# Natural token order for the attention queries, whole-tile output transfers, and more accumulation banks for layer 2's first products

## The chip, the cores and the metric

The kernel runs on one core of one Trainium2 chip. The metric is the device time of one execution in microseconds (us). Three executions of the kernel before gave 834.37, 836.23 and 836.92 us; the median is 836.23 us.

## The reference, cut to what matters

Nystroem attention over 4 batches, 8 heads, 576 tokens and 64 channels a head is followed by two feed-forward layers over the 2304 tokens (512 channels, 2048 hidden).

```python
q_lm = q.reshape(B, H, 32, S // 32, D).mean(axis=3)     # landmarks: means of 18 tokens each
k_lm = k.reshape(B, H, 32, S // 32, D).mean(axis=3)
A, Bm, C = sm(q, k_lm), sm(q_lm, k_lm), sm(q_lm, k)     # softmaxes of scaled products
Z = ...                                                 # 6 Newton steps towards the inverse of Bm
x = (A @ Z @ C @ v).transpose(0, 2, 1, 3).reshape(2304, 512)
h = x @ moe_w_in;   x = (h * tanh(softplus(h))) @ moe_w_out      # layer 1 (Mish)
h = x @ moe2_w_in;  out = (h * sigmoid(h)) @ moe2_w_out          # layer 2 (SiLU)
```

The result is 2304 rows of 512 numbers, 2 KB a row, in the order (batch, token).

## The kernel before, in words

**Order of the work.** Nothing is scheduled on the chip. While the program is built, a planner (`Line`) keeps an estimated time for each engine, runs generators ("chains") by rank and due time, and so writes each engine's instructions down in one fixed order. Each engine then runs its own list in order and waits on semaphores. The planner counts a transfer as its bytes at a fixed rate plus 2.1 us; what it costs a queue to issue one is not in its estimates. SyncE (SP) issues nearly all transfers, in order; a few at the very end are issued by ScalarE (ACT).

**Attention.** Eight groups (4 batches, 2 halves of the heads) are worked one after another. A group's tokens are loaded with landmark l on the partition: token 18 l + 2 j + e of a head lies at partition l of that head, j from 0 to 8, e from 0 to 1. `transposed` turns them by TensorE (three 128x128 blocks into one PSUM bank) and copies each bank, 384 numbers a partition, to an SBUF tile (`Tk` for keys, `Tq` for queries; in the trace group 1 uses pieces named `wp`). Before the change this tile is laid out by (j, head, l). `scores` reads it as the moving operand, 288 columns for each of 8 matmuls a set: queries as 9 runs of 32 columns, keys with the steps of the pattern that `c_side` asks for, in which neighbouring columns lie 384 numbers (1536 bytes) apart. In groups 2 and 3 (`SUMMED`) the landmarks' sums are made from the same tiles by nine matmuls against `twice`; in the other groups they come from VectorE or GpSimd. The rows of the attention's result, and with them the columns of all later activations, follow the order of the query scores' columns: (batch, e, j, l) before.

**Layer 1** multiplies hidden blocks of 128 with 288 tokens; its output goes to DRAM (`ys`) and comes back for layer 2 by `inputs` in three tiles of 768 tokens. `inputs` makes four loads a tile, two into `xs` buffers and two into `wst` buffers (the ring that also takes weights); the loads of tile t+1 are issued while tile t is worked. The first VectorE instruction on them is the subtraction of the two loads in `wst`.

**Layer 2** replaces 8 products of blocks by 7 (`PRODUCTS`). A turn is one pair of hidden blocks: 7 products of 6 matmuls with 384 columns each (`first_products`, names `h<-...` in the trace), and for the pair of the turn before 12 units of 3 matmuls with 512 columns (`second_products`, names `y<-...`). There are 8 turns in each of 3 tiles. In the first turn of all there is no pair before, so the 7 products stand alone. Each takes a PSUM bank from the ring `h_r`, which has two banks; `combined` adds the banks up on VectorE (`z<-h,z`) and only then gives the bank back. The ring `y_r` has four banks from layer 1 and two more in layer 2; one tile's six results collect there.

**Results.** When a tile of 768 tokens is done, `result` copies each of its six banks (128 tokens, 512 numbers) to one of four SBUF buffers `ysb`, and `send` writes it to the result as four transfers of 32 tokens, because 32 neighbouring columns are the 32 landmarks of one (e, j), 18 tokens apart. In the last tile VectorE copies the left half and ScalarE the right half of a bank, and the four transfers are issued in turn by SP and ACT.

Of the kernel before, what the change touches and what calls it, by code (L numbers as in the profile page):

```python
# [35 lines left out]
    S=(2, 0.2, 0.05),  # L36
# [308 lines left out]
class Ring:  # L345
# [12 lines left out]
    def any(self):  # L358
        return any(p[1] for p in self.pools)
# [47 lines left out]
def kernel(  # L407
# [512 lines left out]
    def first_products(t, turn, p):  # L920

        for name, n in PRODUCTS:
            await_(lambda: h_r.any() and (t, name) in x_t and (t, p, name) in f_t)
            bank = h_r.take([128, 512], FP32)
            x, w_ = x_t[t, name], f_t.pop((t, p, name))
            for k in range(2):
                for m, (i, j) in enumerate(PASSES):
                    T.matmul(
                        out=bank[0][:, 0:TH],
                        lhsT=w_[0][:, i, k * 128:k * 128 + 128],  # L930
                        rhs=x[:, k, j],
                        start=(k == 0 and m == 0),
                        stop=(k == 1 and m == 2),
                    )
                    if m != 1 and k + m < 3:
                        yield 0, None
            if turn < HF - 1 or t == NB[2] - 1:
                Ring.give(w_)
            else:
                f_t[t + 1, p, name] = w_  # L940
            if turn == HF - 1:
                marks.add(("x", t, name))
            yield n, combined(t, p, name, bank)
# [110 lines left out]
    def result(t, d):  # L1054

        y_ = y_t[2, t][d]
        yield from until(ysb_r.any)
        ysb_ = ysb_r.take([128, DM], FP32)
        if t < NB[2] - 1:
            VA.copy(out=ysb_[0], in_=y_[0])  # L1060
        else:
            for i, e in enumerate((V, A)):
                e.copy(out=ysb_[0][:, 256 * i:256 * i + 256], in_=y_[0][:, 256 * i:256 * i + 256])
        Ring.give(y_)
        yield "W"
        send(t * 2 * TH // 128 + d, ysb_[0])
        Ring.give(ysb_)

    def send(r, ysb):

        for i in range(128 // LM):
            b, n = divmod(r * (128 // LM) + i, J)
            e, j = divmod(n, J2)
            rows = out[b * S:(b + 1) * S, :].rearrange("(l j e) d -> e j l d", e=2, j=J2)[e, j]
            late = r * 128 >= NT - 2 * TH and i % 2
            line.transfer(nc.scalar if late else nc.sync, out=rows, in_=ysb[i * LM:(i + 1) * LM, :])


    actx = ctx.enter_context(ExitStack())
    qkv_p = actx.enter_context(tc.tile_pool(name="qkv", bufs=2, side="right"))  # L1080
# [10 lines left out]
    class Group:  # L1091
# [55 lines left out]
        def transposed(self, nm, src):  # L1147
            g = self.g
            if g == 1:
                t = self.borrowed["qk".index(nm) + 1][0][:, 0:J].rearrange("p (j a) (c l) -> p j (a c) l", a=2, l=LM)  # L1150
            else:
                t = t_p.tile([128, J2, HG, LM], FP32, tag="T" + nm, name="T" + nm)
            self.tT[nm] = t
            for j in range(0, J2, 3):
                yield from until(self.banks.open)
                pt = self.banks.take([128, 3, 128], FP32)
                for i in range(3):
                    T.transpose(
                        out=pt[0][:, i, :],
                        in_=src[:, 2 * (j + i):2 * (j + i) + 2, :].rearrange("p a d -> p (a d)"),  # L1160
                        identity=ident,
                    )
                yield "W"
                VA.copy(out=t[:, j:j + 3].rearrange("p j h l -> p j (h l)"), in_=pt[0])
                Ring.give(pt)
                if j + 3 < J2:
                    yield "T+"
            yield "W"
            marks.add((g, "T" + nm))
# [15 lines left out]
        def main(self):  # L1185
            g = self.g
            if g in SUMMED:

                yield from until(marked((g, "Tk"), (g, "Tq")))
                yield from until(self.banks.open)  # L1190
                pl = self.banks.take([128, 2, 128], FP32)
                for i, nm in enumerate("kq"):
                    yield from until(marked((g, "T" + nm)))
                    for j in range(J2):
                        T.matmul(
                            out=pl[0][:, i, :],
                            lhsT=twice,
                            rhs=self.tT[nm][:, j].rearrange("p h l -> p (h l)"),
                            start=(j == 0),
                            stop=(j == J2 - 1),  # L1200
                        )
                    marks.add((g, "lm" + nm))
                    if not i:
                        yield "T"
            else:
                yield from until(marked((g, "lmk"), (g, "lmq")))
                yield from until(self.banks.open)
                pl = self.banks.take([128, 2, 128], FP32)
                for i, nm in enumerate("kq"):
                    lm = self.lm[nm].rearrange("p a d -> p (a d)")  # L1210
                    T.transpose(out=pl[0][:, i, :], in_=lm, identity=ident)
# [143 lines left out]
        def c_side(self):  # L1355
            g = self.g
            yield from until(marked((g, "lmT"), (g, "Tk")))
            yield from until(lambda: self.pairs.open(2))
            kT = self.tT["k"]
            s_, s_c = self.scores(  # L1360
                1, lambda e, h: kT[64 * e:64 * e + 64, :, h, :].rearrange("p (c w) l -> p w l c", c=VC)
            )
            marks.add((g, "sc"))
            yield "V+"
            nm2 = s_p.tile([128, 2], FP32, tag="nm2", name="nm2")
            for e in range(2):
                V.tensor_reduce(out=nm2[:, e:e + 1], in_=s_c[e], axis=AX.X, op=ALU.max)
            yield "V"
            nmc = s_p.tile([128, 1], FP32, tag="nmc", name="nmc")
            V.tensor_reduce(out=nmc, in_=nm2, axis=AX.X, op=ALU.max, negate=True)  # L1370
            yield "A+"
            e_c = a_p.tile([128, 2, SH], FP32, tag="ec", name="ec", bufs=2)
            scr = s_p.tile([128, 1], FP32, tag="scr", name="scr")
            scm = s_p.tile([128, 1], FP32, tag="scm", name="scm")
            sc2 = s_p.tile([128, 2], FP32, tag="sc2", name="sc2")
            for e in range(2):
                A.activation(out=e_c[:, e], in_=s_c[e], func=ACTF.Exp, bias=nmc, accum_out=sc2[:, e:e + 1])
                Ring.give(s_[e])
            line.add(self.total(scm, sc2, scr), self.kind("N"), "V", line.end + 0.17)
            yield "T+"  # L1380
            yield from until(lambda: g == 0 or (g - 1, "cv") in marks)
            ect = a_p.tile([96, VI, 128], FP32, tag="ect", name="ect")
            for i0 in (0, 3):
                yield from until(self.banks.open)
                pe = self.banks.take([96, 3, 128], FP32)
                for i in range(i0, i0 + 3):
                    T.transpose(
                        out=pe[0][:, i - i0, :], in_=e_c[:, i % 2, 96 * (i // 2):96 * (i // 2) + 96], identity=ident
                    )
                yield "W"  # L1390
                VA.copy(out=ect[:, i0:i0 + 3, :], in_=pe[0])
                Ring.give(pe)
                yield "T+"
            yield from until(self.banks.open)
            pu_ = self.banks.take([128, D], FP32)
            pu = pu_[0]
            for i in range(VI):
                for h in range(HG):
                    T.matmul(
                        out=pu[32 * h:32 * h + 32],  # L1400
                        lhsT=ect[:, i, 32 * h:32 * h + 32],
                        rhs=self.vn[:, h, i, :],
                        start=(i == 0),
                        stop=(i == VI - 1),
                    )
            marks.add((g, "cv"))
            yield "V"
            yield from until(lambda: (g, "y") in marks and ("w", scr.name) in line.seen)
            VAs.scaled(out=self.yu[:, LM:], in_=pu, scalar1=scr)
            Ring.give(pu_)  # L1410
            yield "W"
            marks.add((g, "u"))
# [9 lines left out]
        def a_side(self):  # L1422
# [1 line left out]
            yield from until(marked((g, "lmT"), (g, "Tq"), (g, "sc")))  # L1424
            yield from until(lambda: self.pairs.open(2))
            qT = self.tT["q"]
            s_, s_a = self.scores(0, lambda e, h: qT[64 * e:64 * e + 64, :, h, :])
            marks.add((g, "scores"))
            if g == 1:
                for t_ in self.borrowed:  # L1430
# [211 lines left out]
```

## Time and profile before

| what | value |
|---|---|
| median of three executions | 836.23 us (834.37 to 836.92) |
| the profiled execution | 835.47 us |
| its span, first to last instruction | 833.3 us |
| TensorE busy | 814.3 us |
| VectorE, ScalarE, GpSimd busy | 560.2, 441.8, 119.5 us |
| mean granted TensorE clock | 0.996 of full speed |

Times in the trace count from the span's start. Attention runs until about 205 us, with layer 1's first work between; layer 1 runs until about 444 us; layer 2 from there. All engines' instructions carry line 262 (the helper that issues them) and all transfers line 274, so they are told apart by the names of their tiles.

### The profile page before, as it was taken

Reading aid. Unit: us, or ns where it says so; the run is one execution under the profiler, and the core shown is the slowest. Engines: PE = TensorE matmul, PEld = TensorE weight load, DVE = VectorE, ACT = ScalarE, POOL = GpSimd, SP = SyncE. Lnnn points to the kernel's source line nnn. Section 1 sums busy time; section 2 is a strip of 40 time slices with the busy share of each in tenths; the row PEclk is TensorE's granted clock in tenths of the full one; section 3 lists DMA queues with packets and bytes.
Section 4 is the critical chain, followed back from the end, with each engine's and each line's share of the span. In section 5 each row is a group of like instructions: output and inputs, shape, how many; then the busy total and the mean of one; then the engine's idle time right before and its main releaser. Section 6 shows DMA issues by size and latency. Waiting matters only on the chain.

```text
span 833.3 us, 15450 instructions
## 1 busy us (share of the span) xinstructions
PE 814.3 (98%) x5920; PEld 729.4 (88%) x5920; DVE 560.2 (67%) x1281; ACT 441.8 (53%) x979; POOL 119.5 (14%) x163
## 2 busy tenths in 40 slices
PE   9999999999999999999998999999999999999997
PEld 7787879878899899999997889888788988988985
DVE  7978875775676879653549998576555567555542
ACT  6466657867566554543436665446445436544422
POOL 2011221030000001000001212211232211232210
PEclk9999999999999999999999999999999999999999
DMA  8784124200175556421143342003100000200002
GB/s 280 234 212 159 58 66 135 87 3 29 32 227 162 183 190 210 145 61 58 57 133 130 103 139 64 0 1 105 48 1 0 1 1 24 53 0 1 1 1 76
DMA packets 41610, 72.30 MB, mean 87 GB/s; under 512 B 4417, under 2 KB 31041, under 8 KB 41537
## 3 DMA queue, kind: packets, MB, share of 16 engines
q1 hardware_dynamic: 40960, 70.53, 27.0%
q8 instruction: 46, 0.75, 0.4%
q10 hardware_dynamic: 576, 0.79, 0.3%
q14 instruction: 28, 0.22, 0.1%
HBM read 57.15 MB, written 14.16 MB: 86 GB/s over the span
## 4 chain that ended last, share of the span: by engine, by line
PE 89%; DVE 5%; DMA 2%; ACT 2%; issue 1%; SPq 0%; ACTq 0%; DVEq 0%
PE y L262 48%; PE h L262 32%; PE t L262 9%; DMA out_dram<-ysb 1%; DMA aw<-in_moe_w_in_dram 1%; DVE m L262 1%; ACT wp L262 1%; DVE z L262 1%; SPq L274 0%; DVE wa L262 0%; DMA kn<-in_k_dram 0%; ACT z L262 0%; ACT ysb L262 0%; ACT L262 0%; DVE xg L262 0%
## 5 line engine op out<-in xcount | busy, mean ns | idle before, releaser
L262 PE MATMUL y<-g,wo 128*128 128x288 f32 x1536 | 227.4, 300 | 1.2 <-DVE g L262 1.1
L262 PEld LDWEIGHTS y<-g,wo 128*128 128x128 f32 x1536 | 208.4, 188 | 13.8 <-issue 11.2
L262 PE MATMUL y<-wo,xg 128*128 128x512 f32 x693 | 180.4, 395 | 0.0
L262 PEld LDWEIGHTS y<-wo,xg 128*128 128x128 f32 x693 | 128.8, 188 | 21.1
L262 DVE TENSOR_TENSOR z<-h,z 128x384 f32<-128x384 f32 x162 | 88.4, 555 | 72.5 <-PE h L262 68.9
L262 PE MATMUL h<-at,wp 128*128 128x288 f32 x768 | 120.0, 301 | 2.7 <-ACT z L262 2.4
L262 PEld LDWEIGHTS h<-at,wp 128*128 128x128 f32 x768 | 105.5, 188 | 12.0 <-issue 7.1
L262 ACT ACTIVATE z<-h 128x288 f32<-128x288 f32 x128 | 51.4, 413 | 65.9 <-PE h L262 64.8
L262 DVE TENSOR_TENSOR g<-z,g 128x288 fp32r<-128x288 f32 x119 | 52.9, 459 | 35.1 <-ACT g L262 31.4
L262 ACT ACTIVATE z<-z 128x384 f32<-128x384 f32 x94 | 49.4, 525 | 32.4 <-DVE z L262 31.9
L262 PE MATMUL h<-xg,wp 128*128 128x384 f32 x288 | 58.1, 336 | 2.3 <-DVE z L262 2.3
L262 PE MATMUL h<-xg,wf 128*128 128x384 f32 x288 | 57.8, 336 | 0.0
L262 PEld LDWEIGHTS h<-xg,wp 128*128 128x128 f32 x288 | 51.2, 188 | 6.2 <-DVE z L262 3.1
L262 DVE TENSOR_TENSOR xg<-z,xg 128x384 fp32r<-128x384 f32 x75 | 42.1, 561 | 20.4 <-ACT xg L262 20.3
L262 ACT CAST g<-z 128x288 fp32r<-128x288 f32 x122 | 50.4, 435 | 8.9 <-PE y L262 7.6
L262 PEld LDWEIGHTS h<-xg,wf 128*128 128x128 f32 x288 | 51.2, 188 | 3.4 <-DVE z L262 0.3
L262 DVE SCALAR_TENSOR_TENSOR m<-wst,m 128x512 int32<-128x512 int32 x64 | 45.3, 708 | 0.7
L262 PE MATMUL y<-wo,wp 128*128 128x512 f32 x171 | 45.2, 396 | 0.0
L262 ACT ACT_TABLE_LOAD x31 | 39.8, 1283 | 8.7 <-DVE nmc L262 3.6
L262 POOL TENSOR_TENSOR g<-z,g 128x288 fp32r<-128x288 f32 x9 | 7.4, 822 | 223.2 <-PE y L262 127.8
L262 ACT CAST xg<-z 128x384 fp32r<-128x384 f32 x75 | 38.4, 513 | 1.5
L262 POOL TENSOR_TENSOR wf<-m,wf 128x256 fp32r<-128x256 f32 x18 | 13.4, 743 | 171.6 <-ACT wf L262 169.9
(237 smaller groups left out, 1171.9 us busy)
## 6 DMA issues: line engine op xcount, KB each, us to landing
wst<-in_moe_w_out_dram SPq DMA_DIRECT2D x32, 512.0 KB, 6.1
wst<-in_moe_w_in_dram SPq DMA_DIRECT2D x22, 512.0 KB, 5.4
kn<-in_k_dram SPq DMA_DIRECT2D x8, 576.0 KB, 6.8
vn<-in_v_dram SPq DMA_DIRECT2D x8, 576.0 KB, 7.1
yh<-ysb SPq DMA_DIRECT2D x32, 144.0 KB, 1.8
ysb<-yh SPq DMA_DIRECT2D x32, 144.0 KB, 2.6
ys<-ysb SPq DMA_DIRECT2D x32, 144.0 KB, 2.2
qn<-in_q_dram SPq DMA_DIRECT2D x7, 576.0 KB, 4.2
```

Of the source, the lines that this page charges most:

```text
L262: r = getattr(self.nc[e], name)(**kw)
```

## The change

1. `transposed` lays the tiles out otherwise. Keys go to (head, w, l, c), so that the scores read 288 neighbouring numbers; the copies write with a step of 3 numbers (12 bytes). Queries go to (head, l, w, c), natural token order within e; the scores read 288 neighbouring numbers and the copies write with a step of 9 numbers (36 bytes). `main` and the two score calls index the new layout; the sums of groups 2 and 3 then read with steps of 3 and 9 numbers.
2. `send` writes what is one run of neighbouring tokens of one (batch, e) in one transfer, every second row of the result: 128 rows where a tile of 128 lies within 288, else two. In tiles 0 and 1 that is one or two transfers of whole rows after the copy, by SP. In tile 2 each half of the columns has its own transfers (1 KB a row): SP's after VectorE's copy, ACT's after ScalarE's.
3. `first_products` may take banks of `y_r` too, in the first turn of the first tile only.

```diff
     def first_products(t, turn, p):
         for name, n in PRODUCTS:
-            await_(lambda: h_r.any() and (t, name) in x_t and (t, p, name) in f_t)
-            bank = h_r.take([128, 512], FP32)
+            rings = (h_r, y_r) if t == turn == 0 else (h_r,)
+            await_(lambda: any(r.any() for r in rings) and (t, name) in x_t and (t, p, name) in f_t)
+            bank = next((r for r in rings if r.ready()), next(r for r in rings if r.any())).take([128, 512], FP32)
...
         if t < NB[2] - 1:
             VA.copy(out=ysb_[0], in_=y_[0])
+            Ring.give(y_)
+            yield "W"
+            send(nc.sync, t * 2 * TH // 128 + d, ysb_[0], 0, DM)
         else:
-            for i, e in enumerate((V, A)):
+            for i, (e, queue) in enumerate(((V, nc.sync), (A, nc.scalar))):
                 e.copy(out=ysb_[0][:, 256 * i:256 * i + 256], in_=y_[0][:, 256 * i:256 * i + 256])
-        Ring.give(y_)
-        yield "W"
-        send(t * 2 * TH // 128 + d, ysb_[0])
+                if i:
+                    Ring.give(y_)
+                send(queue, t * 2 * TH // 128 + d, ysb_[0], 256 * i, 256)
         Ring.give(ysb_)
 
-    def send(r, ysb):
-        for i in range(128 // LM):
-            b, n = divmod(r * (128 // LM) + i, J)
-            e, j = divmod(n, J2)
-            rows = out[b * S:(b + 1) * S, :].rearrange("(l j e) d -> e j l d", e=2, j=J2)[e, j]
-            late = r * 128 >= NT - 2 * TH and i % 2
-            line.transfer(nc.scalar if late else nc.sync, out=rows, in_=ysb[i * LM:(i + 1) * LM, :])
+    def send(queue, r, ysb, at, n):
+        done = 0
+        while done < 128:
+            be, first = divmod(r * 128 + done, SH)
+            rows = min(128 - done, SH - first)
+            to = out[be // 2 * S:be // 2 * S + S, at:at + n].rearrange("(n e) d -> e n d", e=2)[be % 2, first:first + rows]
+            line.transfer(queue, out=to, in_=ysb[done:done + rows, at:at + n])
+            done += rows
...
         def transposed(self, nm, src):
-                t = self.borrowed["qk".index(nm) + 1][0][:, 0:J].rearrange("p (j a) (c l) -> p j (a c) l", a=2, l=LM)
+                t = self.borrowed["qk".index(nm) + 1][0][:, 0:J].rearrange("p j d -> p (j d)")
-                t = t_p.tile([128, J2, HG, LM], FP32, tag="T" + nm, name="T" + nm)
+                t = t_p.tile([128, J * D], FP32, tag="T" + nm, name="T" + nm)
+            if nm == "k":
+                t = t.rearrange("p (h w l c) -> p c w h l", h=HG, w=J2 // VC, c=VC)
+            else:
+                t = t.rearrange("p (h l w c) -> p w c h l", h=HG, w=VC, l=LM)
...
-                VA.copy(out=t[:, j:j + 3].rearrange("p j h l -> p j (h l)"), in_=pt[0])
+                VA.copy(out=t[:, j // 3], in_=pt[0].rearrange("p w (h l) -> p w h l", h=HG))
...
-                            rhs=self.tT[nm][:, j].rearrange("p h l -> p (h l)"),
+                            rhs=self.tT[nm][:, j // 3, j % 3],
...
-                1, lambda e, h: kT[64 * e:64 * e + 64, :, h, :].rearrange("p (c w) l -> p w l c", c=VC)
+                1, lambda e, h: kT[64 * e:64 * e + 64, :, :, h].rearrange("p c w l -> p w l c")
...
-            s_, s_a = self.scores(0, lambda e, h: qT[64 * e:64 * e + 64, :, h, :])
+            s_, s_a = self.scores(
+                0, lambda e, h: qT[64 * e:64 * e + 64, :, :, h].rearrange("p w c l -> p l w c")
+            )
```

## Rows read from the trace of the kernel before

**Rows 1.** The page, busy time of each engine: us (share), instructions.
```profile
PE 814.3 (98%) x5920; PEld 729.4 (88%) x5920; DVE 560.2 (67%) x1281; ACT 441.8 (53%) x979; POOL 119.5 (14%) x163
```

**Rows 2.** Timeline where layer 2 begins: start, us, engine, out<-in, count, [idle before <-releaser].
```profile
444.02 1.22 PE L262 MATMUL h<-x,wf 128*128 128x384 f32 x6
...
448.99 1.31 PE L262 MATMUL h<-xg,wp 128*128 128x384 f32 x6 [0.40 <-DVE z L262]
...
452.44 1.32 PE L262 MATMUL h<-wp 128*128 128x384 f32 x6 [1.09 <-DVE z L262]
...
453.91 1.32 PE L262 MATMUL h<-x,wp 128*128 128x384 f32 x6
```

**Rows 3.** Windows at layer 2's start: span, busy PE, PEld, DVE, ACT, POOL, PEclk.
```profile
450.00:452.00 2.00, 1.35 (x8) 1.03 (x6) 2.00 (x6) 1.20 (x3) 0.03 (x1) 1.00 0.90 327
```

**Rows 4.** Timeline of SP's queue where tile 0's results leave.
```profile
576.89 0.38 SPq L274 DMA_DIRECT2D wst<-ys  x1
577.37 5.60 SPq L274 DMA_DIRECT2D out_dram<-ysb  x12
583.07 0.38 SPq L274 DMA_DIRECT2D wst<-ys  x1
```

**Rows 5.** Timeline of the compute engines there.
```profile
579.57 0.57 ACT L262 COPY ysb<-y 128x512 f32<-128x512 f32 x1
...
585.83 1.56 PE L262 MATMUL y<-wo,wp 128*128 128x512 f32 x6
586.95 0.56 DVE L262 TENSOR_TENSOR wst<-wst 128x384 f32<-128x384 f32 x1 [3.50 <-DMA out_dram<-ysb]
...
588.69 0.55 DVE L262 TENSOR_TENSOR z<-h,z 128x384 f32<-128x384 f32 x1
...
589.30 1.31 PE L262 MATMUL h<-xg,wp 128*128 128x384 f32 x6 [1.91 <-DVE z L262]
```

**Rows 6.** Windows just after it, columns as in rows 3.
```profile
591.00:592.00 1.00, 1.00 (x4) 0.80 (x3) 1.00 (x3) 0.54 (x2) 0.74 (x1) 0.50 0.00 0
```

**Rows 7.** Chain of waits, 570 to 597 us: start, us, what.
```profile
571.67 1.04 PE h L262 x6
572.71 1.41 PE y L262 x6
...
590.61 2.29 PE y L262 x6
592.90 1.72 PE h L262 x6
```

**Rows 8.** Timeline of the last results.
```profile
824.20 0.37 ACT L262 COPY ysb<-y 128x256 f32<-128x256 f32 x1 [5.79 <-DVE ysb L262]
...
824.60 5.67 SPq L274 DMA_DIRECT2D out_dram<-ysb  x12
...
824.96 0.89 ACTq L274 DMA_DIRECT2D out_dram<-ysb  x2
...
829.16 1.75 ACTq L274 DMA_DIRECT2D out_dram<-ysb  x4
```

**Rows 9.** Timeline of group 4's attention, 100 to 120 us.
```profile
105.77 0.47 ACT L262 COPY Tq<-t 128x384 f32<-128x384 f32 x1
...
107.20 0.88 PE L262 MATMUL t<-Tk,lmT 64*32 64x288 f32 x16
...
114.15 0.71 PE L262 MATMUL t<-Tq,lmT 64*32 64x288 f32 x16
```

**Rows 10.** Timeline of group 3's landmark sums of queries.
```profile
69.66 2.17 PE L262 MATMUL t<-Tq,twice 128*128 128x128 f32 x18
```

**Rows 11.** Groups by line and form: count | busy us, mean ns | idle before.
```profile
L262 DVE TENSOR_REDUCE lmk<-kn 128x64 f32<-128x1152 f32 x5 | 11.0, 2193 | 2.9 <-DMA kn<-in_k_dram 2.9
...
L262 DVE TENSOR_REDUCE asm<-at 128x18 f32<-128x576 f32 x8 | 6.0, 748 | 0.8 <-ACT at L262 0.7
```

**Rows 12.** Transfers: out<-in, queue, count, KB each, median us to landing.
```profile
yh<-ysb SPq DMA_DIRECT2D x32, 144.0 KB, 1.8
```

## The prediction

> **What bounds the kernel now.** The page's busy times come first: TensorE is busy 98% of the span, 814.3 of 833.3 us [rows 1]. So nothing on another engine counts unless TensorE waits for it, and all that can be won is in three places: some 19 us in which TensorE is idle, stretches in which its clock is low, and the time after its last product. I then read the chain of waits and the timeline at the places where TensorE stands still, and find three that the change touches.
>
> The first is layer 2's first turn. Seven products of six matmuls run from 444.02 to 453.91 us, where the next turn's first begins [rows 2]: 9.89 us. In steady state six such matmuls take 1.04 us [rows 7], so seven need 7.28. Lost: 2.6 us, of which 0.40 and 1.09 are waits that the timeline names, for `z<-h,z` on VectorE, the instruction that frees a bank of `h_r` [rows 2]. The reader is also to see that VectorE has no gap there: 2.00 us busy of 2.00 between 450 and 452 [rows 3].
>
> The second is at 587 to 594 us. VectorE stands 3.50 us before it subtracts `wst<-wst` at 586.95; its next instructions include the `z<-h,z` of 588.69, and TensorE waits 1.91 us for that, until 589.30 [rows 5]. The row blames a result transfer. But the subtraction needs two loads, and the second sits on SP's queue behind twelve result transfers that take 5.60 us to issue; it goes out at 583.07, right behind them [rows 4]. It lands when the subtraction starts, 3.88 us after its issue began. The data are tile 2's and not urgent, but the instruction is in VectorE's fixed order, and all that TensorE needs next is queued behind it. After the idle time the granted clock is 0.50, the 1.2 GHz level, where it was 1.00 (2.4 GHz) [rows 6], and the chain of waits shows the price: six matmuls of 512 columns take 2.29 us instead of 1.41, six of 384 columns 1.72 instead of 1.04 [rows 7].
>
> The third is the tail. The last results are copied from 824 us on; SP needs 5.67 us to issue twelve transfers, and ACT issues its last four from 829.16 for 1.75 us, to 830.91 [rows 8], while the span ends at 833.3. Two on ACT take 0.89, so 0.44 each.
>
> **The first turn's banks.** The edit adds no instruction; it takes the bank out of the condition. The gain is at most 2.6 us. It is at least 0: VectorE is full [rows 3], and the second turn's products still go to `h_r` alone, so the wait may only move from the third product to the eighth. I take 1.5, the two named waits, because the seven products need no more from VectorE to be issued, and each sum then finds its product ready; what is late next is the next turn's first product, behind VectorE's sums, by the remaining 1.1.
>
> **Tile 0's results.** 24 transfers become 8 (tiles of 128 tokens that cross a multiple of 288 need two; among the first six these are the third and the fifth). SP's queue is otherwise in the same order. Between the two loads it now holds 1 + 2 + 1 transfers instead of 12. The fourth bank's copy starts at 579.57 and takes 0.57 [rows 5], so its transfer goes at about 580.2 and, at 0.47 an issue (5.60 / 12), the load at about 580.65: 2.4 us earlier. Landing 3.88 later it is there at 584.5. VectorE then waits some 1.1 instead of 3.5, and the `z<-h,z` ends at 588.69 + 0.55 - 2.4 = 586.8. TensorE's product before that ends at 585.83 + 1.56 = 587.39 [rows 5], so it finds the sum done. It gains the wait of 1.91, the restart (1.31 - 1.04 = 0.27), and, as the clock has no idle time to fall after, 0.88 + 0.68 = 1.56 of slow matmuls: 3.7 us together. Bounds: 0, if the load stays late, to 3.7. At 2.4 us earlier there are 0.6 us to spare, so I take the whole. Tile 1's results (24 transfers become 8 too) have no such load between them: covered, nothing.
>
> **The tail.** Twelve transfers a queue become eight (two of the last six tiles cross). ACT has six copies of 0.37 and now eight issues of 0.44 instead of twelve: at most 4 x 0.44 = 1.8 us less. But before, an issue ran beside the next tile's copy (the pair at 824.96 sits between copies); now each waits for the copy just ahead of it, some 0.37 that was partly hidden, and with four `ysb` buffers the fifth tile still waits for the first one's transfers. The transfers themselves, 128 KB in pieces of 1 KB, are bounded by a neighbour of 144 KB in rows of 1152 bytes that lands in 1.8 us [rows 12]: no worse than now. Bounds 0 and 1.8, taken 0.9.
>
> **The new layouts.** A key set of scores, 16 records, takes 0.88 us with far-apart columns, a query set with runs of 32 takes 0.71 [rows 9]. Read as one run, keys should cost what queries do: 8 x 0.17 = 1.4 us less. Against it, the landmark sums of groups 2 and 3 now read with steps; a set takes 2.17 us [rows 10]. The step of 1536 bytes cost a factor 0.88 / 0.71 = 1.24, so a stepped set may cost 0.5 more: 1.0 for the two query sets (36 bytes), another 1.0 for the keys (12 bytes), or nothing. I take the queries' 1.0. Net -0.4; bounds -1.4 and +0.6.
>
> The 48 copies write with steps. No row has such a write. The nearest is a stepped read on VectorE: summing 1152 numbers 256 bytes apart takes 2193 ns, while 576 neighbours take 748 [rows 11], so 1152 would take about 1496; 0.6 ns more a number, or 0.23 us for a copy of 384. All 48: 0 to 11 us of mostly ACT time. I take nothing, for two reasons: a store need not be waited for as a read is, and in the groups' middle the delay is covered. Group 4's last query copy ends at 106.2 and TensorE reads it at 114.15 [rows 9], with other work of its own between. Without that cover it would cost up to 0.23 a copy.
>
> The Trainium skill has a rule against this edit: Advanced Engine Details and Errata, section Memory Cachelines, says that SBUF works in lines of 16 bytes, that at least two accesses must fall on a line to hide its latency, and that a pattern with another line each time pays. By that rule the query copies (36 bytes) and their sums pay, and the key scores gain; rows 9 agree with the second half, and no row shows a stepped write. By that rule the sum would lose 24 x 0.23 = 5.6 us wherever the cover fails; as a mechanism it is the slower rival below.
>
> **Sum.** Against the profiled execution's own 835.47 us (span 833.3 and 2.2 around it): -1.5 - 3.7 - 0.9 - 0.4 = -6.5, so 829.0. The median of the runs shown lies 0.76 above that execution; the predicted median is 829.8.
>
> **The rivals.**
> - The stall at 587 stays. For it: the instruction order is written by a planner that knows nothing of issue times, and its estimates shift with the first turn's banks, so the load may come out elsewhere, or another transfer hold it. Against: the planner counts the same bytes for four transfers as for one, so the order should be kept. Then -2.8: 833.4.
> - The first turn gains nothing, since VectorE is the limit there [rows 3] and the wait moves to the eighth product: 831.3.
> - The change does nothing measurable: both stalls stay in another form, and the tail is bound by bytes. Left is 1.3: about 835.
> - Slower: the stepped copies. If both kinds pay the 0.23 and TensorE waits for each, that is 11.0 us over 205 us of attention, and with the second key sums 12: 836.2 - 6.5 + 12 = 841.7. It decides once 6.5 of these 12 us are exposed. For it: the read row. Against: the cover of rows 9, and ACT's spare time (53% busy over the span, rows 1).
>
> **How the numbers follow.** This kernel's measurement can tell about 0.3%, 2.5 us, from no change: the borders are 833.7 and 838.7. Chances: all parts work, with a partial loss here or there, 0.55 (826.8 to 831.5; its best is 836.2 - 2.6 - 3.7 - 1.8 - 1.4); the stall at 587 stays 0.17, about two thirds of it faster; the first turn gains nothing 0.13; nothing measurable 0.08; slower 0.07. Faster 0.55 + 0.11 + 0.13 = 0.79; same 0.06 + 0.08 = 0.14; slower 0.07. The range reaches from the best case to the case with the stall and a little more: 826.5 to 834.
>
> **What would show it.** Right: no named wait between the first seven products, whose span falls from 9.9 to about 8.4 us; the second `wst<-ys` some four issues behind the first; VectorE's wait before `wst<-wst` near 1 us; the clock at 1.00 after it; key and query score sets both near 0.71; ACT's last issue within about 6 us of its first copy. Wrong: `Tq<-t` copies well above 0.47 us with TensorE waits for them before 205 us; a TensorE wait for a `y` bank in the second turn; VectorE still 3 us late at the subtraction; a low clock elsewhere. Most likely to break it is a new order of VectorE's work in layer 2 that puts another early load in its way.

## The result and the profile after

The changed kernel takes 841.79 us (median of six executions, 841.30 to 842.50); the kernel before took 835.42 beside it (six executions, 833.52 to 836.92). The ratio is 1.0078 [1.0063, 1.0092]: slower, where 829.8 was forecast and 834.0 was the upper end. The profiled execution has a span of 839.5 us against 833.3.

Where the time went is read from stages, by the start of the same instruction in both traces:

| stage | before | after | difference |
|---|---|---|---|
| start to the first query scores | 12.36 | 13.37 | +1.01 |
| from there to layer 2's first product | 431.66 | 441.45 | +9.79 |
| layer 2's first turn | 9.89 | 9.32 | -0.57 |
| second turn of tile 1 (the tenth of all) | 19.47 | 15.70 | -3.77 |
| all other turns, 22 of them | 350.37 | 350.37 | 0.0 |
| first copy of the last results to the end | 9.58 | 9.34 | -0.24 |

A turn is timed from the first matmul of its first product to that of the next turn. The stall of [rows 5] lies in the tenth turn, whose first product starts at 579.53 before. The differences add up to 6.22 us, the spans' own. Layer 2 gave 4.6 us; everything lost was lost before it. The first line can't be put down to the change: in six traces with the attention as before (that of before and five of the experiments) it lies between 12.26 and 13.92. The second lies between 431.66 and 432.62 there.

Busy times of the page after, as in [rows 1]:

```profile
PE 819.7 (98%) x5920; PEld 732.7 (87%) x5920; DVE 562.5 (67%) x1280; ACT 451.5 (54%) x977; POOL 122.2 (15%) x166
```

TensorE has the same 5920 instructions and 5.4 us more of busy time; ScalarE has 9.7 us more. So instructions became longer. The groups by form say which (out<-in, count | busy us, mean ns | idle before):

```profile
L262 ACT COPY Tq<-t 128x384 f32<-128x384 f32 x20 | 17.6, 882 | 2.2 <-PE t L262 2.0
...
L262 ACT COPY Tk<-t 128x384 f32<-128x384 f32 x18 | 12.5, 694 | 8.4 <-PE t L262 8.3
...
L262 PE MATMUL t<-Tq,twice 128*128 128x128 f32 x36 | 8.6, 409 | 0.0
...
L262 PE MATMUL t<-Tk,twice 128*128 128x128 f32 x36 | 6.6, 343 | 0.0
```

The same four groups of before had 484, 480, 275 and 275 ns. Now the timeline after: group 2's landmark sums, answering [rows 10], and group 4's scores, answering [rows 9]:

```profile
47.12 3.25 PE L262 MATMUL t<-Tk,twice 128*128 128x128 f32 x18
...
50.47 4.32 PE L262 MATMUL t<-Tq,twice 128*128 128x128 f32 x18
...
116.96 0.72 PE L262 MATMUL t<-Tk,lmT 64*32 64x288 f32 x16
...
123.72 0.71 PE L262 MATMUL t<-Tq,lmT 64*32 64x288 f32 x16
```

A set of sums was 2.17 us; keys now take 3.25, queries 4.32, in each of two groups: 2 x (1.08 + 2.15) = 6.5 us, all of it time in which TensorE itself works. Key scores fell from 0.88 to 0.72, seven sets of them after the first query scores: -1.2. Of the 9.79 us that leaves 9.79 - 6.5 + 1.2 = 4.5 us (4.2 by 432.0, the mean of those six traces) for the copies, which became 24 x 0.40 + 24 x 0.21 = 14.7 us longer in all. How they reach TensorE is in part seen in its waits by releaser, of the first 212 us (us in total, times, longest; those that ScalarE released after the first query scores):

```profile
PE t L262 <- ACT ec L262: 0.5, 2, 0.3
PE t L262 <- ACT ut L262: 0.5, 1, 0.5
...
PE t L262 <- ACT Tq L262: 0.4, 2, 0.2
...
PE h L262 <- ACT yu L262: 0.4, 1, 0.4
...
PE t L262 <- ACT Tk L262: 0.2, 1, 0.2
PE h L262 <- ACT eb L262: 0.2, 1, 0.2
```

Together 2.2 us; before there were two such rows, `yu` 0.3 and `ec` 0.2. Only 0.6 of it names a slower copy: the rest names other results of ScalarE, whose list the copies are part of. But idle time is the small part of the second line. Windows over that stretch, before and after, columns as in [rows 3], then the weight loads' waits for the copies there after; before they were 0.7 for `Tq` and 0.9 for `Tk`:

```profile
12.36:444.02 431.66, 424.07 (x3973) 381.60 (x3958) 302.93 (x779) 246.67 (x560) 32.46 (x36) 1.00 0.39 124
13.37:454.82 441.45, 432.59 (x3973) 387.34 (x3958) 303.48 (x779) 254.63 (x561) 32.43 (x36) 1.00 0.38 121
```
```profile
PEld t L262 <- ACT Tq L262: 2.5, 10, 0.4
...
PEld t L262 <- ACT Tk L262: 1.8, 6, 0.5
```

TensorE's busy time rises by 8.5 us and its idle time by 1.3. Sums and key scores are 5.3 of the 8.5; the other 3.2 lie in matmuls that do the same work as before, so part of the waiting isn't idle time of TensorE and shows in the weight loads ahead of the matmuls. The matmuls of this stretch come in the same order in both traces, so the time from each one's start to the next one's can be compared. Outside the sums and scores these times grew by 4.6 us together: by 2.2 where the next matmul or its weights waited (over 0.15 us) for a copy of `Tq` or `Tk`, by 0.9 where they waited for another result of ScalarE, and the rest is scattered, with no wait of this size.

Layer 2's start in the timeline, answering [rows 2]:

```profile
454.82 1.22 PE L262 MATMUL h<-x,wf 128*128 128x384 f32 x6
...
457.96 1.20 PE L262 MATMUL y<-xg,wf 128*128 128x384 f32 x6
...
464.14 1.33 PE L262 MATMUL h<-x,wp 128*128 128x384 f32 x6 [1.42 <-DVE z L262]
```

The waits of 0.40 and 1.09 are gone, a `y` bank is in use, and one wait of 1.42 has appeared before the eighth product, the first that may not use that ring.

Where tile 0's results leave, SP's queue, answering [rows 4]; VectorE there, answering [rows 5]; and windows, columns as in [rows 3], answering [rows 6]:

```profile
585.40 0.43 SPq L274 DMA_DIRECT2D wst<-ys  x1
586.74 2.80 SPq L274 DMA_DIRECT2D out_dram<-ysb  x4
589.63 0.40 SPq L274 DMA_DIRECT2D wst<-ys  x1
```
```profile
593.90 0.56 DVE L262 TENSOR_TENSOR wst<-wst 128x384 f32<-128x384 f32 x1 [1.21 <-DMA wst<-ys]
```
```profile
590.00:595.00 5.00, 5.00 (x27) 4.60 (x26) 2.75 (x7) 3.21 (x8) 0.73 (x1) 1.00 0.80 241
```

Four issues lie between the two loads instead of twelve; VectorE waits 1.21 instead of 3.50; TensorE has no gap, and its granted clock stays at 1.00.

The last results in the timeline, answering [rows 8]:

```profile
830.66 0.37 ACT L262 COPY ysb<-y 128x256 f32<-128x256 f32 x1 [5.79 <-DVE ysb L262]
...
835.00 1.18 ACTq L274 DMA_DIRECT2D out_dram<-ysb  x2
835.07 0.42 DVE L262 COPY ysb<-y 128x256 f32<-128x256 f32 x1 [1.04 <-ACT ysb L262]
836.23 0.37 ACT L262 COPY ysb<-y 128x256 f32<-128x256 f32 x1 [1.25 <-DVE ysb L262]
836.63 0.34 ACTq L274 DMA_DIRECT2D out_dram<-ysb  x1
```

From the first copy of ScalarE to its last issue's end it is 6.31 us, where it was 6.71. VectorE's last copy now waits 1.04 for ScalarE, and ScalarE's last copy 1.25 for VectorE's.

### The profile page after: what moved, and what is told of

It reads as the page before. It is cut to its first block, busy times and chain, and to the rows that moved or that the text cites. A ratio compares the mean times of both kernels' runs of the same rounds, so it can differ in the third digit from the quotient of the medians.

```text
span 839.5 us, 15401 instructions
## 1 busy us (share of the span) xinstructions
PE 819.7 (98%) x5920; PEld 732.7 (87%) x5920; DVE 562.5 (67%) x1280; ACT 451.5 (54%) x977; POOL 122.2 (15%) x166
## 4 chain that ended last, share of the span: by engine, by line
PE 91%; DVE 4%; ACT 3%; DMA 1%; issue 1%; ACTq 0%; SPq 0%; DVEq 0%
PE y L262 49%; PE h L262 33%; PE t L262 9%; ACT wp L262 1%; DMA kn<-in_k_dram 1%; DVE at L262 1%; DVE m L262 0%; ACT Tq L262 0%; ACT z L262 0%; ACT Tk L262 0%; ACT L262 0%; DVE g L262 0%; DVE st L262 0%; ACTq L274 0%; DVE lmk L262 0%
```

## The experiments

**The theory** after the result (theory S in the expectations): a step between neighbouring numbers costs the engine that makes it, at either end, by how many numbers of a 16-byte piece of SBUF it uses: the sums pay as readers, the copies as writers. **A rival**, called theory C in the expectations: the writes alone pay, and the sums are long only because their copies come late. **Another**: little of it is the layout; what layer 2's edits should have gained went elsewhere.

### Keys as before, queries as before, both

Three kernels from the changed one, each with old storage; the scores keep their column orders, so with old query storage they read numbers 512 bytes apart.

```diff
-                t = t.rearrange("p (h w l c) -> p c w h l", h=HG, w=J2 // VC, c=VC)
+                t = t.rearrange("p (c w h l) -> p c w h l", h=HG, w=J2 // VC, c=VC)
```
```diff
-                t = t.rearrange("p (h l w c) -> p w c h l", h=HG, w=VC, l=LM)
+                t = t.rearrange("p (w c h l) -> p w c h l", h=HG, w=VC, l=LM)
```

> The changed kernel with the keys stored as before (copies write neighbours, scores read 1536 bytes apart); queries as changed. Theory S (every access with a step costs in place: key copies 0.69 instead of 0.48 us, key sums 3.25 instead of 2.17 us a set): the two key sums give back 2.2 us and the key copies about 1.3, the eight key score sets cost 1.3 again: 841.8 - 2.2 = 839.6 us. Theory C (the loss is ScalarE's time for copies; the sums are late only because the copies are): the 24 key copies are a third of the added copy time, so a third of 10.8 us comes back less 1.3: 839.5 us, but with key sums still above 2.17 us a set.

Keys as before (first diff): 839.23 us, 1.0057 [1.0042, 1.0072], about what both theories gave; what tells them apart is the sums. The kernel before had 834.81 beside it in this and the next three runs. The timeline of group 2's sums:

```profile
47.15 2.17 PE L262 MATMUL t<-Tk,twice 128*128 128x128 f32 x18
...
49.42 4.32 PE L262 MATMUL t<-Tq,twice 128*128 128x128 f32 x18
```

The sums of keys are back at 2.17; those of queries stay at 4.32 although nothing of theirs was touched.

> The changed kernel with the queries stored as before and read by the scores in natural order, 512 bytes apart from one column to the next; keys as changed. Theory S: query sums give back 4.3 us, query copies about 3, the eight query score sets cost 0.16 each more, as the keys' did: 841.8 - 7.3 + 1.3 = 835.8 us, query sums at 2.17 us a set and query score sets at 0.88. Theory C: two thirds of 10.8 come back, less 1.3: 835.9 us; what tells them apart is where TensorE falls behind, in the sums or before them.

Queries as before (second diff): 838.52, 1.005 [1.0035, 1.0065], 2.7 us above what was expected. The timeline of group 2:

```profile
46.02 3.24 PE L262 MATMUL t<-Tk,twice 128*128 128x128 f32 x18
...
62.33 1.39 PE L262 MATMUL t<-Tq,lmT 64*32 64x288 f32 x16
```

The sums do as the theory says: keys 3.24, queries back at 2.17. The miss is in the last row: scores that take their columns in turn from nine runs cost 1.39 a set, not the 0.88 of the keys' three runs. Eight sets are 5.4 us where 1.3 were counted; the rest of the kernel gave 1.4 back.

> The changed kernel with both tiles stored as before; only the scores read queries in natural order, 512 bytes apart; output transfers and banks as changed. Theory S and theory C: all 10.8 us come back, the query score sets cost 8 x 0.16: 841.8 - 10.8 + 1.3 = 832.3 us, faster than the kernel before (835.4). A third theory, that the order of the tokens or the output transfers are themselves to blame, expects it to stay slower than before, above 838.

Both as before: 836.38, 1.0023 [1.0013, 1.0033], missed by eight sets at 1.39. From the first query scores to layer 2 it is 437.43 us. That is 4.8 to 5.8 us over the old attention, and the eight query sets, all of them behind that mark, with 0.68 more each are 5.4 of it: between -0.6 and 0.4 is left of the 9.8, which is within the spread, so with the storage goes the loss. Layer 2 stands as in the kernel after (first turn 9.32, tenth 15.70, tail 9.40).

The copies' share follows from the first two in the same way, against the 432.0 us of the old attention. Keys as before: 438.80, less 4.3 for the sums of queries, leaves 2.5 for the copies of queries. Queries as before: 438.97, less 2.15 for the sums of keys and 5.4 for the scores, plus 1.2 for the keys', leaves 0.6 for the copies of keys. Together 3.1, beside the 4.2 to 4.6 above; each of these remainders carries the spread of up to 1.0 us of an unchanged attention.

### Old storage in the two summed groups only

```diff
-                t = t.rearrange("p (h w l c) -> p c w h l", h=HG, w=J2 // VC, c=VC)
+                t = t.rearrange("p (c w h l) -> p c w h l" if g in SUMMED else "p (h w l c) -> p c w h l", h=HG, w=J2 // VC, c=VC)
...
-                t = t.rearrange("p (h l w c) -> p w c h l", h=HG, w=VC, l=LM)
+                t = t.rearrange("p (w c h l) -> p w c h l" if g in SUMMED else "p (h l w c) -> p w c h l", h=HG, w=VC, l=LM)
```

> The changed kernel with both tiles stored as before in groups 2 and 3 alone, where the landmark sums read them; groups 0, 1 and 4 to 7 as changed. Theory S: the four sums give back 6.5 us and the copies of the two groups about 2.1; four score sets cost 0.16 each again: 841.8 - 8.0 = 833.8 us. Theory C: a quarter of the copies, so a quarter of 10.8 us: 839.1 us.

835.43, 1.0006 [0.9997, 1.0016]. Both sums are at 2.17 although the copies of the other six groups are slow as in the kernel after: theory C, with 839.1, falls. The time is 1.6 us above the 833.8 of the first theory; the two groups' query scores, which again come from nine runs, are 1.0 of that (0.68 more a set where 0.16 was counted).

### The step by itself

A small kernel of its own: ScalarE copies 384 and VectorE 192 numbers a partition into a tile with steps of 1 to 16 numbers; TensorE reads 192 columns with the same steps, then 288 columns in turn from 2, 3 and 9 runs that lie 1536 bytes apart. The copies run beside matmuls of the same kernel; only the last groups of matmuls have TensorE to themselves.

> Not the reference's work: copies of a PSUM bank to SBUF with steps of 1, 2, 3, 4, 5, 8, 9 and 16 numbers (384 a partition on ScalarE, 192 on VectorE), matmuls of 192 columns that read SBUF with these steps, and matmuls whose columns go round 2, 3 or 9 runs 1536 bytes apart; nothing else is computed. If a line of 16 bytes costs two accesses' time however little of it is used, the cost of a number follows the lines touched: step 2 free, step 3 at 1.5 times, steps of 4 and more at 2 times and equal; for a matmul 192 columns at those factors. If the cost rises with the step itself, 9 costs more than 4 and 16 more than 9. If only powers of two are bad (banks), 8 and 16 stand out. Runs taken in turn: each column touches another line, so 2 times for all three by the first theory, though the keys' scores before (three runs) took only 1.24 times.

ScalarE's copies with steps 1, 2, 3, 4 and 9 (ns lowest/median/highest of four), then TensorE's groups of 15 matmul records (two records a matmul) with the same steps from the timeline, then those from 2, 3 and 9 runs:

```profile
L44 ACT COPY act<-src x4: 478/478/478, 32.5 to 34.1; 128x384 f32<-128x384 f32 x4
...
L44 ACT COPY act<-src x4: 497/502/512, 34.4 to 36.0; 128x384 f32<-128x384 f32 x4
...
L44 ACT COPY act<-src x4: 666/667/671, 36.4 to 38.5; 128x384 f32<-128x384 f32 x4
...
L44 ACT COPY act<-src x4: 832/835/836, 39.0 to 41.6; 128x384 f32<-128x384 f32 x4
...
L44 ACT COPY act<-src x4: 843/848/899, 49.0 to 51.6; 128x384 f32<-128x384 f32 x4
```
```profile
32.49 2.60 PE L54 MATMUL pe<-big,ident 128*128 128x192 f32 x15
...
35.10 2.71 PE L54 MATMUL pe<-big,ident 128*128 128x192 f32 x15
...
37.89 4.02 PE L54 MATMUL pe<-big,ident 128*128 128x192 f32 x15
...
42.07 5.28 PE L54 MATMUL pe<-big,ident 128*128 128x192 f32 x15
...
58.55 5.35 PE L54 MATMUL pe<-big,ident 128*128 128x192 f32 x15
...
69.24 4.76 PE L61 MATMUL str<-big,ident 128*128 128x288 f32 x15
...
74.17 5.13 PE L61 MATMUL str<-big,ident 128*128 128x288 f32 x15
...
79.61 7.48 PE L61 MATMUL str<-big,ident 128*128 128x288 f32 x15
```

A step of 2 is nearly free (478 and 502 ns; 2.60 and 2.71 us), 3 costs TensorE 1.5 times as much, and 4 and 9 twice; longer ones cost no more (TensorE 5.33 and 5.05 us with 5 and 16, ScalarE 858 and 844 ns with 8 and 16). A copy grows by 0.19 us with step 3 and 0.37 with step 9; in the kernel it was 0.21 and 0.40. VectorE's copies of 192 go the same way: 357, 357, 418, 506 and 506 ns. An access is slow by its own step and not by its neighbour's: VectorE's 357 ns without a step were taken beside matmuls with a step of 8.

The Trainium skill's rule in Advanced Engine Details and Errata, section Memory Cachelines (lines of 16 bytes, two accesses wanted on each), agrees with these rows. The page gives no price; if each line touched is taken to cost the time of two accesses, steps of 1 and 2 put four and two numbers on a line and are free, a step of 3 has 0.75 lines a number and costs 0.75 / 0.5 = 1.5, and a step of 4 or more has one line a number and costs 2.0. TensorE measured 1.04, 1.55, 2.03 and 2.06 for steps of 2, 3, 4 and 9; a whole copy on ScalarE, part of whose time does not grow with the numbers copied (256 take 372 ns, 512 take 586), 1.05, 1.40, 1.75 and 1.77. Several runs in turn are milder than the rule would make them: one run of 288 columns would take an estimated 2.60 x 288 / 192 = 3.9 us, so 2 and 3 runs cost 1.22 and 1.32 times as much, 9 runs 1.92. Without a step all these records take 0.90 ns a column. Layer 2's take 0.45 (1.04 us for 6 of 384), and no run shows what a step does to those.

### The banks alone, and what the stall is worth

The kernel before with the third edit alone:

```diff
-            await_(lambda: h_r.any() and (t, name) in x_t and (t, p, name) in f_t)
-            bank = h_r.take([128, 512], FP32)
+            rings = (h_r, y_r) if t == turn == 0 else (h_r,)
+            await_(lambda: any(r.any() for r in rings) and (t, name) in x_t and (t, p, name) in f_t)
+            bank = next((r for r in rings if r.ready()), next(r for r in rings if r.any())).take([128, 512], FP32)
```

> The kernel before with the first turn's banks alone; layouts, token order and output transfers as before. Theory S (the banks give 0.6 us, the 3.8 us at 587 come from fewer transfers ahead of the second load): 834.8 - 0.6 = 834.2 us, and VectorE's late subtraction and TensorE's wait with it stay. Rival: the banks shift the planner's order so that the load no longer stands behind the results, and the 3.8 us are theirs: 830.4 us.

834.05, 0.9988 [0.9978, 0.9998], the kernel before at 834.84 in this and the next two runs. The first turn takes 9.33 as in the kernel after. VectorE's wait is as it was, and this time the row names the load itself:

```profile
587.12 0.56 DVE L262 TENSOR_TENSOR wst<-wst 128x384 f32<-128x384 f32 x1 [3.48 <-DMA wst<-ys]
```

Its tenth turn is 17.77: in this execution the clock did not fall after the gap, so the stall cost 2.1 us where it cost 3.8 in the profile of before.

### Old token order, whole-tile transfers

To have the fewer transfers without the layouts: old storage and old token order, each transfer's destination written as up to 4 groups of 32 rows (only the lines of the transfers are shown).

```diff
-            to = out[be // 2 * S:be // 2 * S + S, at:at + n].rearrange("(n e) d -> e n d", e=2)[be % 2, first:first + rows]
+            to = out[be // 2 * S:be // 2 * S + S, at:at + n].rearrange("(l j e) d -> e j l d", e=2, j=J2)[
+                be % 2, first // LM:(first + rows) // LM
+            ]
...
```

> The changed kernel with both tiles stored and read as before, so that results come in the old token order; banks as changed; a run of results of one (batch, e) still goes out in one transfer, whose rows in DRAM then follow (j, landmark) in two steps, 2 rows and 36 rows apart... in place of one. Theory S: the 10.8 us of the attention come back whole and the 0.6, 3.8 and 0.3 us of the other parts stay: 834.8 - 4.7 = 830.1 us. Rival: a transfer with four blocks of 32 rows lands later than one with 128 rows in one step, so the tail, or the second load, gives some of it back: 832 to 834.

861.52, 1.0315 [1.0297, 1.0333]: a miss by 31 us, and not in the attention, which is as before (431.74 us). The tenth turn is 26.27, the same turn of tile 2 is 19.73 instead of 15.68, and the tail 24.56. SP's queue in the timeline, then windows in this kernel's tail and in the tail of the kernel after (the last two numbers are the DMA engines' mean busy share and GB/s):

```profile
576.75 5.69 SPq L274 DMA_DIRECT2D out_dram<-ysb  x4
```
```profile
844.00:848.00 4.00, 0.00 (x0) 0.00 (x0) 0.42 (x1) 0.37 (x1) 0.00 (x0) 0.50 0.27 95
```
```profile
833.00:835.00 2.00, 0.67 (x3) 0.19 (x1) 0.42 (x1) 0.98 (x3) 0.00 (x0) 1.00 0.85 290
```

The same bytes move at a third of the rate with a third of the engines' share, so the four buffers come free late and ScalarE, VectorE and TensorE wait behind them. The Trainium skill has this in DMA: Bandwidth & Descriptors, in the section on why a DMA increments its semaphore by 16: a transfer is spread over as many engines, up to 16, as divide the slowest dimension of both sides. With 4 groups outermost that is 4 of 16, and the share of 0.27 agrees. The trace's DMA records speak for it and against slower packets: in both tails most packets have 1024 bytes, and a packet takes 49 ns on average here and 46 in the kernel after, but here mostly four or five are under way at a time, there mostly 13 to 18.

> As e9_old_order, but the second turn of the first tile may take banks of the larger ring too. If VectorE's sums are what the eighth product waits for because VectorE has no time left (busy without a gap there): no change against e9_old_order, within 0.5 us; TensorE's 1.4 us only move on. If it waits for a bank alone: 1.4 us less.

The same kernel with `t == 0 and turn < 2`: 858.51, 1.028 [1.0264, 1.0295]. The first turn falls from 9.33 to 7.74 and the second rises from 15.78 to 16.06: 1.3 us gained, at 1.4 expected if the bank is the limit. (The rest of the 3.0 us lies mainly in the two turns that wait for results, 26.04 and 18.15 instead of 26.27 and 19.73.) VectorE's first four sums start at the same times in both, 2.65, 4.92, 8.73 and 9.3 to 9.5 us after the turn's start; so it is the bank that the eighth product waits for.

### The stall without the layouts

The banks-alone kernel, with the loads' first subtractions placed later in VectorE's order by the planner; the transfers stay 72. Of its diff, the lines that delay the subtraction:

```diff
+            if t:
+                late = line.now + 5.0
+                yield from until(lambda: line.now >= late)
```

> The kernel before with the first turn's banks, and with the planner told to wait 5 us after the loads for tiles 1 and 2 before it places VectorE's first subtraction on them; layouts and the 72 output transfers as before. If the 3.8 us at 587 come from that one instruction standing in VectorE's order before its load has landed: VectorE does not wait, the clock stays, 834.05 - 3.7 = 830.3 us, though SP issues as many transfers as before. If the number of transfers matters in itself (their bytes, their time on SP): 834.

832.61, 0.9969 [0.9958, 0.998]; the kernel before had 834.97 beside it in this and the next three runs. SP's queue and VectorE in the timeline:

```profile
578.48 5.74 SPq L274 DMA_DIRECT2D out_dram<-ysb  x12
584.32 0.39 SPq L274 DMA_DIRECT2D wst<-ys  x1
```
```profile
590.33 0.94 DVE L262 TENSOR_TENSOR wst<-wst 128x384 f32<-128x384 f32 x1
```

The load is as late as ever, behind twelve issues; VectorE no longer waits for it, and the tenth turn falls to 15.93. So the stall was VectorE's fixed order in front of a late load, and it can be taken away at either end. The gain over the banks alone is 1.4 us, not the 3.7 expected; in that kernel's profile the clock did not fall, so only 2.1 us were there to be won.

> As e11_later, with banks of the larger ring for the first two turns. The run with both turns' banks on another base took 1.3 us less for these two turns: 830.3 - 1.3 = 829.0 us, against 834.8 before. If VectorE was the limit after all, 830.3.

With the banks for two turns as well: 829.59 (829.36 to 830.54), 0.9941 [0.9928, 0.9953]. The turns are 7.71, 15.67 and, the tenth, 15.70, and of TensorE's waits from 440 us on one row is left, which is layer 1's:

```profile
PE y L262 <- DVE g L262: 0.6, 1, 0.6
```

It beats both kernels, with the storage, the token order and the 72 transfers of the kernel before.

### Natural order without long steps

The kernel after with the banks for two turns, keys stored as before, and queries stored so that two of the three `w` lie side by side and the third apart. Copies write with steps of 2 and 1; a head's scores are two matmuls, of 192 and 96 columns, that write PSUM in natural order.

```diff
+                pairs = t[:, 0:768].rearrange("p (c n w) -> p w c n", c=VC, w=2)
+                t = [pairs[:, 0], pairs[:, 1], t[:, 768:1152].rearrange("p (c n) -> p c n", c=VC)]
...
+                    (to[:, :, :, 0:2], both[r, :, n].rearrange("p c l w -> p l c w")),
+                    (to[:, :, :, 2], single[r, :, n].rearrange("p c l -> p l c")),
```

> The changed kernel with natural token order, banks for two turns, keys stored as before, and queries in another layout: two neighbours of six of a landmark's nine queries lie side by side (copies write with a step of 2), the other three are stored apart (copies write neighbours); each head's scores are two matmuls, of 192 and 96 columns, that write their PSUM columns in natural order. Theory of lines (a step of 2 is free): query copies at 0.50 us, sums at 2.2 us a set, score sets near 0.9: attention about 1.6 us later than before, the rest 5.9 us earlier, 830.5 us. Rival: stepped writes to PSUM and twice the matmuls cost what the stepped reads did (1.39 us a set): 834.3 us.

831.61, 0.9962 [0.9949, 0.9976], 1.1 us above what was expected. The group of the copies, and a set of scores from the timeline:

```profile
L262 ACT COPY Tq<-t 128x384 f32<-128x384 f32 x20 | 10.1, 506 | 2.8 <-PE t L262 2.5
```
```profile
116.17 0.83 PE L262 MATMUL t<-Tq,lmT 64*32 64x192 f32 x32
```

Copies (506 ns) and sums (2.19 a set) cost about what they did in the old storage, with the kernel after's token order and transfers: the loss was the step, not the order. The scores are 0.12 longer a set, 1.0 us for eight, and the stretch from the first query scores to layer 2 is 433.04 us, 1.0 over the old attention's mean.

> As e13_pairs, with two more result buffers at the end (two of the weights' decode buffers), so that the fifth and sixth of the last copies do not wait for earlier transfers. If the buffers are why the tail got only 0.3 us shorter: 0.6 to 1.0 us less than e13_pairs. If ACT's own sequence (copy, issue, copy, issue) sets it: the same.

The same with two more result buffers in the last tile (`spare = t == NB[2] - 1 and not ysb_r.ready() and ms_r.ready()`): 831.35, 0.9962 [0.9949, 0.9976], the tail 9.59 instead of 9.76. Buffers aren't what holds the tail.

## Why the prediction was wrong

**The step that failed** is "The new layouts", taken at -0.4 with bounds of -1.4 and +0.6; it was +9.8.

- *The landmark sums.* Foreseen was 1.0 us, from the factor 1.24 by which key scores exceeded query scores [rows 9]. That factor belongs to three runs read in turn; the steps here are 36 and 12 bytes, and the runs showed 2.0 and 1.5 (4.32 and 3.25 over 2.17). 6.5 us, the larger part.
- *The 48 copies.* They were taken as nothing, with a bound of 0.23 a copy. They cost 0.40 and 0.21. "A store need not be waited for as a read is" had no row behind it and fell outright: a stepped write makes its instruction longer as a stepped read does. "In the groups' middle the delay is covered" held for some two thirds: 3 to 4.6 of the 14.7 us reached TensorE. The cover was judged by when group 4's query tile is read. That left out the weight loads that wait for a copy in other places, and that ScalarE works its list in order, so that other results of it (`ec`, `ut`, `eb` above) come later too.
- *The key scores* did as predicted: 0.88 to 0.72.

The slower rival had the price almost to the microsecond (841.7), but by another sum, so that was luck: it gave the copies 11 and the sums 2 in all (the queries' 1.0 in the base and the keys' 1.0), where the copies cost TensorE 3 to 4.6 and the sums 6.5, and it counted on 6.1 us from layer 2, which gave 4.6. (The best case in the working adds up to 826.7, not 826.8; nothing hangs on it.) Its chance of 0.07 was too low: the nearest row, the stepped sum on VectorE [rows 11], pointed to it, and was set against an argument that no row supported.

**Tile 0's results** were right in each link: four issues between the loads, VectorE's wait of 1.21 where 1.1 was worked out, TensorE's sum ready, the clock at 1.00, and 3.77 us gained at 3.7. The rival "the stall at 587 stays" did not come. That the size fits to 0.1 us is partly luck: 1.6 of the 3.7 is the low clock of the one execution that was profiled, and in the kernel with the banks alone the same wait cost 2.1 us in all.

**The first turn's banks** had the right mechanism and the wrong size: -0.57 for -1.5. The working let 1.1 us move to the next turn's first product; it was 1.42, and the rest of the turn gave less. That it was the bank and not VectorE was shown by the kernel with two turns, whose first turn is 7.74.

**The tail** gave 0.24 for 0.9, within its bounds. The fear that each issue waits for the copy ahead of it was right; ScalarE's last issue ends 6.31 us after its first copy instead of 6.71, although it issues eight transfers instead of twelve. The gain itself is hardly clear of the spread: the old tail takes 9.58 to 9.79 us in four traces, the new one 9.34 to 9.76 in six.

So layer 2's three steps gave 4.6 of 6.1 us, and the layouts took twice that. Open is the way of the last third of the copies' 4.6 us, for which the trace names no wait, and the size itself, as an unchanged attention differs by up to 1.0 us from run to run.

## What to carry to other kernels

Before a layout is turned so that one reader gets neighbouring numbers, count the 16-byte pieces that every writer and every other reader of the tile touches for each number: up to half a piece a number was nearly free here, and a whole one doubled a plain matmul and made a copy, which pays as a writer, 1.75 times as long. Take the price of a step from a row with that same step, and when only a farther row exists, let its price stand in the sum rather than argue it away. A late transfer in front of an engine with a fixed order can be cured where it waits as well as where it is issued; here a few lines in the planner's order gave what a new token order was meant to give.

## What the runs showed of the hardware that was not expected

- A stepped write makes its instruction longer, as a stepped read does: ScalarE 478, 502, 667, 835 and 848 ns for 384 numbers with steps of 1, 2, 3, 4 and 9; TensorE's moving operand 2.60, 2.71, 4.02, 5.28 and 5.35 us for 15 reads of 192.
- Columns taken in turn from a few far runs are cheap: 1.22 times for two runs, 1.32 for three, 1.92 for nine (against an estimate for one run), so a distance of 1536 bytes between neighbours can cost less than one of 12.
- A transfer whose destination had 4 as its outermost dimension ran with a DMA share of 0.27 at 95 GB/s; one run of rows had 0.85 at 290 GB/s.
- After nearly the same gap of TensorE, 1.91 and 1.81 us, the granted clock fell to 0.50 in one execution and stayed at 1.00 in another, so one stall cost 3.8 us or 2.1.
